# Attention and gated convolution on one core: the convolution's middle tap moved into the sigmoid's scale, the norm's gain into x, first loads on another queue, a new order, and unread products in TensorE's early waits

## The chip, the cores and the metric

The kernel runs on one core of a Trainium2 chip. The metric is device time in microseconds (us), as the median of several runs. The core has a TensorE (matrix products, PE in the profile), a VectorE (DVE), a ScalarE (ACT), a GpSimd (POOL) that here issues most loads, and a SyncE (SP) that here issues transfers only. Each engine takes its instructions strictly in its own order and waits on semaphores for others. Matrix products are written to PSUM, eight banks of 2 KB per partition; everything else lives in SBUF, 128 partitions wide.

## What is computed

Eight batches, 8 heads, 576 positions, 64 numbers per head, so a model width of 512; the gated layer is 1024 wide.

```
kv  = einsum('bhsd,bhse->bhde', k, v)            # no softmax
o   = einsum('bhsd,bhde->bhse', q, kv)
o   = o / sqrt(mean(o*o, -1) + 1e-6) * g_norm    # per head, g_norm has 64 entries
x   = o.transpose(0, 2, 1, 3).reshape(8, 576, 512)
h   = relu(x @ w_in)                             # 512 -> 1024
c   = w0*h[s-1] + w1*h[s] + w2*h[s+1]            # per feature, zero at both ends
out = (h * sigmoid(c)) @ w_out                   # 1024 -> 512
```

All inputs and the output are fp32; inside, operands of products are bf16.

## The kernel before

Everything is kept transposed, features on partitions and positions along the free axis: a batch of x is 4 tiles of 128 x 576, a batch of h is 8 tiles of 128 x 576. The kernel is a set of small steps, each a function with one to a dozen instructions, and a text, ORDER, that lists them one after another by name and numbers (`hm.3.4` is step `hm` for batch 3, feature tile 4). A loop at the end runs through that text, so the order of the instructions on each engine is written out by hand; dependencies between engines are found by the framework, and a buffer pool hands out buffers in turn, waiting until the oldest of its kind is free. Names and lines that matter below:

- `load` (line 148): q, k, v of a batch through GpSimd's queue, which converts fp32 to bf16 on the way. Batch 0 takes q whole and k, v by two heads. `load_w_in` (158): w_in in three parts, kept fp32 in `w_stage`, one of them through SyncE; `ws` (261, VectorE) multiplies by g and converts to `w_in_sb`. `Lw` (256) loads w_out.
- `kv` (272): 64 x 64 products per head pair, 12 per pair and tile; `kvc` (284, 286) copies them into a block-diagonal `kvbd`. `qt` (296) transposes q on TensorE, 24 products per step; `qc` (303, VectorE) copies out. `ot` (308, 309) makes o, 64 and 512 columns.
- Batch 0 has its own norm: `sq` (326), `on` (a product with a matrix of ones), `nl` (348, reciprocal root on ScalarE), `mu0` (357, the product into x, reading in a strided order). The later batches: `sq` (328) and `oc` (334) on ScalarE, `ss` (373), `ln` (383), `sl` (391 to 394, VectorE), `sp` (403, TensorE spreads the factor over 128 partitions), `mu` (409, VectorE: x = o times the factor).
- `hm` (426): eight products of 288 columns into `h_ps`; `re` (432, ScalarE): relu to h.
- The convolution goes by six groups of batches, CONV: 0; 1; 2 and 3; 4 and 5; 6; 7. Batch 0 ('P') runs on TensorE: `di` (480) builds 24 diagonal matrices, `cv` (492) multiplies with them, six products per feature tile, `sv` (500) is the sigmoid, `mv` (506) the gating product. The others ('D') run on VectorE by pairs of feature tiles: `ta` (451) makes three scaled copies of h per tile, `ad` (458, 459) adds them with a shift of one position, `sg` (465, ScalarE) is one sigmoid per pair, `mg` (471) multiplies h in place. Two `tap` buffers take turns.
- `om` (516): eight products of 512 columns per 128 output rows, `ea` (522, ScalarE) copies out, `st` (532) stores through SyncE. Batches go in twos here: 9 row blocks for each.
- PSUM: pool 'a' has three tiles of two banks (for `qt`, `ot`, `hm`, `sp`, `cv`), pool 'b' two of one bank (`kv`, `ss`, `om`).

Of the kernel before, what the change touches and what calls it, by code (L numbers as in the profile page):

```python
# [58 lines left out]
CONV = {0: (0, 1, 'P'), 1: (1, 1, 'D'), 2: (2, 2, 'D'), 3: (4, 2, 'D'), 4: (6, 1, 'D'), 5: (7, 1, 'D')}  # L59
BUFS = {'a': 3, 'b': 2, 'q': 2, 'k': 2, 'v': 2, 'qT': 5, 'sq': 8, 'o32': 8, 'xT': 2, 'h': 2, 'tap': 2, 'row': 8, 'w': 2, 'gate': 3}  # L60

ORDER = """
di.4 di.7 di.6 qt.0.0 qc.0.0 qt.0.1 kv.0.0.1 kvc.0.0.1.0 kvc.0.0.1.1 ot.0.0 di.5 kv.0.1.1 sq.0.0 qc.0.1 on.0
di.2 kvc.0.1.1.0 nl.0 kvc.0.1.1.1 ot.0.1 sq.0.1 kv.0.2.1 on.1 kvc.0.2.1.1 mu0.0 kvc.0.2.1.0 di.1 Lk.1
Lv.1 nl.1 kv.0.3.1 ot.0.2 kvc.0.3.1.1 sq.0.2 on.2 kvc.0.3.1.0 nl.2 mu0.1 ot.0.3 sq.0.3 on.3 ws.1 Lq.1
ws.2 mu0.2 nl.3 ws.0 mu0.3 hm.0.0 hm.0.7 re.0.7 re.0.0 kv.1.0.4 kvc.1.0.4.0 Lw hm.0.5 Lk.2 Lv.2 Lq.2
re.0.5 hm.0.2 re.0.2 qt.1.0 kvc.1.0.4.1 hm.0.4 re.0.4 qc.1.0 ot.1.0 qt.1.1 qc.1.1 ot.1.1 sq.1.0 oc.1.1 sq.1.1
ot.1.2 sq.1.2 di.0 ot.1.3 sq.1.3 oc.1.3 oc.1.2 ss.1 ln.0 hm.0.1 Lk.3 re.0.1 Lv.3 hm.0.6 di.3 Lq.3 oc.1.0
hm.0.3 cv.0.0 re.0.6 sl.0 sp.1.0 mu.1.0 re.0.3 sv.0.0 cv.0.4 sp.1.1 kv.2.0.4 sv.0.4 Lk.4 sp.1.3 mu.1.1
kvc.2.0.4.1 mv.0.0 mu.1.3 sp.1.2 mu.1.2 cv.0.6 cv.0.2 sv.0.6 hm.1.0 mv.0.6 qt.2.1 sv.0.2 mv.0.4 mv.0.2 qc.2.1  # L70
kvc.2.0.4.0 hm.1.1 re.1.0 re.1.1 ot.2.3 ta.1.0 cv.0.7 sq.2.3 sv.0.7 hm.1.4 Lv.4 oc.2.3 cv.0.5 qt.2.0 ta.1.1
ad.1.0 re.1.4 sv.0.5 sg.1.0 hm.1.5 re.1.5 qc.2.0 ot.2.1 mg.1.0 cv.0.1 sq.2.1 sv.0.1 oc.2.1 ot.2.0 sq.2.0
oc.2.0 kv.3.0.4 kvc.3.0.4.0 ta.1.4 Lq.4 qt.3.0 qc.3.0 hm.1.6 hm.1.7 kvc.3.0.4.1 ta.1.5 mv.0.7 re.1.6 re.1.7
ot.3.0 oc.3.0 sq.3.0 mv.0.1 qt.3.1 cv.0.3 qc.3.1 ot.3.3 sv.0.3 oc.3.3 ta.1.6 Lk.5 Lv.5 ta.1.7 ot.3.2 sq.3.3
sq.3.2 ot.3.1 oc.3.2 mv.0.3 ot.2.2 kv.4.0.4 sq.3.1 sq.2.2 oc.3.1 hm.1.2 ss.2 re.1.2 ss.3 ad.1.3 ln.1 
kvc.4.0.4.0 Lq.5 qt.4.1 qt.4.0 ad.1.2 mv.0.5 qc.4.1 hm.1.3 qc.4.0 kvc.4.0.4.1 om.0.2 re.1.3 oc.2.2 sl.1 sp.2.0
mu.2.0 sg.1.3 sp.3.2 mu.3.2 sp.2.2 om.0.0 mu.2.2 mg.1.3 sp.2.3 ot.4.2 Lk.6 Lv.6 mu.2.3 ea.0.2 sp.2.1 om.0.3
mu.2.1 oc.4.2 ot.4.3 sq.4.2 ea.0.0 ta.1.2 sp.3.3 mu.3.3 sq.4.3 oc.4.3 sp.3.0 mu.3.0 ta.1.3 kv.5.0.4 sg.1.2
sp.3.1 kvc.5.0.4.0 hm.2.0 hm.2.5 ea.0.3 mu.3.1 ad.1.1 re.2.0 re.2.5 hm.2.4 qt.5.0 kvc.5.0.4.1 re.2.4 qc.5.0
sg.1.1 qt.5.1 qc.5.1 hm.2.2 re.2.2 ot.4.1 oc.4.1 sq.4.1 st.0.0 mg.1.2 hm.3.4 re.3.4 Lq.6 Lk.7 Lv.7 Lq.7 mg.1.1  # L80
hm.3.5 re.3.5 ot.5.3 oc.5.3 sq.5.3 hm.3.2 hm.3.3 re.3.2 ot.5.0 hm.2.3 ta.2.4 re.3.3 sq.5.0 ta.2.5 re.2.3
ot.5.2 sq.5.2 oc.5.0 oc.5.2 om.0.4 ot.4.0 ta.2.2 ot.5.1 hm.3.6 oc.4.0 ad.2.2 ta.2.3 sq.5.1 ea.0.4 sq.4.0
om.0.5 ss.4 ss.5 oc.5.1 re.3.6 qt.6.0 ea.0.5 ln.2 qt.7.0 qt.6.1 ad.2.1 qc.6.0 om.0.8 ea.0.8 sg.2.1 qc.6.1
om.0.1 sl.2 sp.4.0 ea.0.1 sp.4.2 qc.7.0 sp.5.1 kv.6.0.4 mu.4.0 hm.3.0 mu.5.1 mu.4.2 mg.2.1 sp.5.0 hm.3.1
mu.5.0 re.3.0 re.3.1 sp.4.3 kv.7.0.4 kvc.7.0.4.0 kvc.6.0.4.0 sp.5.3 kvc.7.0.4.1 hm.2.1 re.2.1 mu.4.3 ta.2.0
hm.2.6 sp.4.1 st.0.8 mu.5.3 kvc.6.0.4.1 sg.2.2 sp.5.2 ta.2.1 mu.4.1 om.0.7 hm.3.7 re.2.6 ad.2.0 mg.2.2 re.3.7
sg.2.0 mu.5.2 om.0.6 hm.2.7 re.2.7 hm.4.0 ea.0.6 hm.5.1 ta.2.6 re.5.1 hm.4.3 re.4.3 ta.2.7 ea.0.7 hm.5.0
re.5.0 re.4.0 hm.5.5 re.5.5 hm.5.2 re.5.2 st.0.3 ad.2.3 mg.2.0 st.0.7 qt.7.1 hm.4.1 hm.5.4 sg.2.3 re.4.1
qc.7.1 re.5.4 hm.4.5 re.4.5 hm.4.2 ot.6.1 re.4.2 ta.3.0 oc.6.1 hm.5.3 sq.6.1 mg.2.3 ot.6.3 om.1.5 ot.6.0
re.5.3 ot.7.1 oc.6.3 sq.6.3 ea.1.5 ot.6.2 sq.6.0 oc.7.1 om.1.2 ta.3.1 ta.3.2 oc.6.0 ta.3.3 ad.3.0 ot.7.3  # L90
oc.6.2 sq.6.2 ea.1.2 st.0.6 om.1.6 ot.7.0 sq.7.1 hm.4.4 om.1.8 sg.3.0 re.4.4 ea.1.6 sq.7.0 sq.7.3 ot.7.2
st.1.2 ad.3.1 sq.7.2 ea.1.8 oc.7.3 om.1.3 ea.1.3 ss.6 ss.7 ln.3 hm.5.6 st.0.1 mg.3.0 ta.3.4 re.5.6 ta.3.5
ad.3.2 om.1.4 hm.4.7 st.0.5 om.1.0 oc.7.2 sl.3 oc.7.0 st.1.5 sp.6.0 mu.6.0 sp.6.3 re.4.7 mu.6.3 sg.3.1
ea.1.4 hm.4.6 re.4.6 sp.7.0 mu.7.0 hm.5.7 re.5.7 sp.6.2 om.1.7 st.0.4 ea.1.0 mg.3.1 sp.7.3 ea.1.7 mu.6.2
# [14 lines left out]
def kernel(  # L109
# [11 lines left out]
    nc = tc.nc  # L121
# [8 lines left out]
    NF = D_ff // P  # L130
    eps = 1e-6
# [4 lines left out]
    loads = pool("loads", 2)  # L136
    work = pool("work", 2)
    ps_a = pool("ps_a", BUFS["a"], space=PSUM)
    ps_b = pool("ps_b", BUFS["b"], space=PSUM)


    qkv = {}

    def load(name, b, h0=0, n=H):
        src = {"q": q, "k": k, "v": v}[name]
        if (name, b) not in qkv:
            qkv[name, b] = loads.tile([PS, H, R * D], BF16, name=name + "_sb", bufs=BUFS[name])
# [53 lines left out]
    for t in kvbd:  # L201
        nc.vector.memset(t, 0.0)
# [375 lines left out]
```

## Time and profile before

| | us |
|---|---|
| median of 3 runs | 203.81 (203.37 to 204.84) |
| span of the profiled execution | 201.0 |
| TensorE busy | 175.3 (87%) |
| VectorE busy | 155.3 (77%) |
| ScalarE busy | 145.9 (73%) |
| GpSimd busy | 25.4 (13%) |

The span goes from the first to the last instruction of one profiled execution; all durations come from that one. Busy time alone does not say what sets the end: an engine can be full in one stage and wait in another. So three views are read below: slices of the span (a digit is the busy tenth of a slice), the chain of waits followed back from the last instruction (start, length, what), and the busy time of each engine between two points in time. In lists of instructions, `out<-in` gives tiles by name, then partitions x elements and type, then how many were merged into the line (`x6`); the length of a merged line runs from the first start to the last end. Two instructions in a row on one engine overlap a little at their ends, so the distance from start to start is shorter than a duration.

The largest groups, busy us and mean ns of one:

| line, engine | what | number | us | ns |
|---|---|---|---|---|
| 426 PE | h_ps, 288 columns | 512 | 69.9 | 291 |
| 516 PE | om_ps, 512 columns | 278 | 64.1 | 379 |
| 451 DVE | taps, 576 / 1152 elements | 72 / 48 | 22.2 / 21.6 | 371 / 514 |
| 458 + 459 DVE | adds, 1150 / 2300 elements | 24 / 16 | 18.2 / 21.7 | 757 / 1358 |
| 409 DVE | x = o times factor, 576 | 28 | 20.1 | 749 |
| 432 ACT | relu, 576 | 64 | 41.0 | 656 |
| 465 ACT | sigmoid, 1152 / 2304 | 12 / 8 | 14.0 / 17.1 | 1163 / 2138 |
| 492 PE | products with diagonals | 48 | 10.8 | 286 |

### The profile page before, as it was taken

To read this page: it belongs to the slowest core of one execution; us is meant where nothing else is said; L and a number is where in the kernel's file an instruction comes from. 1 tells how busy PE (TensorE), PEld (TensorE's weight loads), DVE (VectorE), ACT (ScalarE), POOL (GpSimd) and SP (SyncE) were. 2 spreads that over 40 slices of the span, in tenths; PEclk is the share of its full clock that TensorE was granted. 3 is DMA by queue.
4 is the path that set the end of the run, shared out by engine and by line. 5 is a ranking of instruction groups with operands and counts; after the bars stand their busy time and mean duration, and the time that the engine had idled before them with its cause. 6 is when DMAs were issued, how large, how long until landed. Compare 5 with 4: busy or idle time off the path is not lost.

```text
span 201.0 us, 4350 instructions
## 1 busy us (share of the span) xinstructions
PE 175.3 (87%) x1783; PEld 111.8 (56%) x1801; DVE 155.3 (77%) x325; ACT 145.9 (73%) x222; POOL 25.4 (13%) x38
## 2 busy tenths in 40 slices
PE   0057299799998999999999999999999999999792
PEld 0043057477775657766575776445667774444340
DVE  3097921458879799799899999989799999999400
ACT  2006516995999979999678899999978865684532
POOL 7373403103132303100000000000000000000000
PEclk9999999999999999999999999999999999999999
DMA  5999999999999999970200020070005001423654
GB/s 120 146 221 306 198 205 205 204 203 204 204 190 185 201 203 207 202 119 3 104 5 3 0 104 3 7 306 2 3 0 209 3 0 51 159 108 118 247 229 188
DMA packets 26295, 27.03 MB, mean 134 GB/s; under 512 B 1292, under 2 KB 21284, under 8 KB 26276
## 3 DMA queue, kind: packets, MB, share of 16 engines
q0 software_dynamic: 20368, 16.78, 52.4%
q1 hardware_dynamic: 5908, 9.98, 13.1%
q8 instruction: 14, 0.23, 0.4%
q14 instruction: 5, 0.04, 0.1%
HBM read 32.52 MB, written 9.44 MB: 209 GB/s over the span
## 4 chain that ended last, share of the span: by engine, by line
PE 59%; DVE 22%; DMA 10%; ACT 5%; issue 2%; POOL 1%; DVEq 0%; POOLq 0%; ACTq 0%
PE h_ps L426 25%; PE om_ps L516 18%; DVE tap L451 8%; DMA w_stage<-in_moe_w_in_dram 5%; DMA q_sb<-in_q_dram 5%; DVE h L471 4%; PE qt_ps L296 4%; DVE tap L459 3%; PE kv_ps L272 3%; PE sp_ps L403 3%; DVE tap L458 3%; PE cv_ps L492 3%; DVE xT L409 2%; PE o_ps L309 2%; ACT tap L465 2%
## 5 line engine op out<-in xcount | busy, mean ns | idle before, releaser
L426 PE MATMUL h_ps<-xT,w_in_sb 128*128 128x288 bf16 x512 | 69.9, 291 | 3.1 <-DVE w_in_sb L261 2.4
L516 PE MATMUL om_ps<-w_out_sb,h 128*128 128x512 bf16 x278 | 64.1, 379 | 1.5 <-DVE h L471 1.0
L426 PEld LDWEIGHTS <-w_in_sb 128*128 128x128 bf16 x512 | 49.9, 99 | 18.8 <-DVE w_in_sb L261 2.5
L432 ACT ACTIVATE h<-h_ps 128x576 bf16<-128x576 f32 x64 | 41.0, 656 | 14.9 <-PE h_ps L426 14.5
L516 PEld LDWEIGHTS <-h 128*128 128x128 bf16 x288 | 28.0, 98 | 32.2 <-DVE h L471 1.5
L451 DVE TENSOR_SCALAR tap<-h,cw 128x576 bf16<-128x576 bf16 (+1 forms) x120 | 43.8, 428 | 1.8 <-ACT h L432 1.3
L522 ACT ACTIVATE row<-om_ps 128x512 f32<-128x512 f32 x36 | 22.1, 618 | 15.6 <-PE om_ps L516 13.1
L465 ACT ACTIVATE tap<-tap 128x1152 bf16<-128x1152 bf16 (+1 forms) x20 | 31.1, 1553 | 1.6 <-DVE tap L459 1.5
L409 DVE TENSOR_TENSOR xT<-o,sp_ps 128x576 bf16<-128x576 f32 x28 | 20.1, 749 | 5.0 <-PE sp_ps L403 4.8
L471 DVE TENSOR_TENSOR h<-h,tap 128x1152 bf16<-128x1152 bf16 (+1 forms) x20 | 19.8, 992 | 1.8 <-ACT tap L465 1.8
L459 DVE TENSOR_TENSOR tap<-tap 128x1150 bf16<-128x1150 bf16 (+1 forms) x20 | 20.1, 1004 | 0.7
L303 DVE COPY qT<-qt_ps 128x1152 bf16<-128x1152 bf16 x16 | 11.8, 754 | 11.1 <-PE qt_ps L296 10.9
L458 DVE TENSOR_TENSOR tap<-tap 128x1150 bf16<-128x1150 bf16 (+1 forms) x20 | 19.8, 991 | 0.0
L328 ACT ACTIVATE sq<-o_ps 128x576 bf16<-128x576 f32 x28 | 18.2, 689 | 0.5 <-PE o_ps L309 0.5
L334 ACT ACTIVATE o<-o_ps 128x576 f32<-128x576 f32 x28 | 18.1, 677 | 0.5 <-ACT row L522 0.5
L286 ACT ACTIVATE kvbd<-kv_ps 64x256 bf16<-64x256 f32 (+1 forms) x18 | 6.0, 339 | 12.2 <-PE kv_ps L272 11.8
L148 POOL DMA_DIRECT2D k_sb<-in_k_dram x11 | 8.0, 723 | 35.9 <-PE kv_ps L272 35.9
L296 PE MATMUL qt_ps<-ident,q_sb 96*64 96x96 bf16 x384 | 11.2, 217 | 1.4 <-DMA q_sb<-in_q_dram 1.1
L296 PEld LDWEIGHTS <-q_sb 96*64 96x64 bf16 x384 | 9.6, 117 | 3.3 <-issue 2.1
L403 PE MATMUL sp_ps<-wparts,spread 128*128 128x288 bf16 x56 | 9.8, 286 | 0.2 <-DVE xT L409 0.2
L272 PEld LDWEIGHTS <-k_sb 96*64 96x64 bf16 x384 | 8.0, 123 | 3.3 <-issue 3.3
L309 PE MATMUL o_ps<-qT,kvbd 128*128 128x512 bf16 x25 | 9.6, 407 | 0.0
(55 smaller groups left out, 114.9 us busy)
## 6 DMA issues: line engine op xcount, KB each, us to landing
out_dram<-row SPq DMA_DIRECT2D x36, 256.0 KB, 2.3
q_sb<-in_q_dram POOLq DMA_DIRECT2D x8, 576.0 KB, 12.6
k_sb<-in_k_dram POOLq DMA_DIRECT2D x7, 576.0 KB, 11.3
v_sb<-in_v_dram POOLq DMA_DIRECT2D x7, 576.0 KB, 13.6
w_stage<-in_moe_w_in_dram POOLq DMA_DIRECT2D x1, 1024.0 KB, 9.9
w_out_sb<-in_moe_w_out_dram POOLq DMA_DIRECT2D x1, 1024.0 KB, 19.9
k_sb<-in_k_dram POOLq DMA_DIRECT2D x4, 144.0 KB, 9.4
v_sb<-in_v_dram POOLq DMA_DIRECT2D x4, 144.0 KB, 9.2
```

Source lines behind the costliest of these rows:

```text
L296: nc.tensor.transpose(ps[i * D:(i + 1) * D, tt, r * PS:(r + 1) * PS], q_sb[:, 2 * (2 * u + tt) + i, r * D:(r + 1) * D], ident[:PS, :PS])
L328: nc.scalar.activation(s.rearrange("p (n r) -> p n r", r=R), natural(src), AX.Square)
L409: nc.vector.tensor_mul(x_tile(b)[:, t, :].rearrange("p (e n) -> p e n", e=2), T["o32", b, t].rearrange("p (e n) -> p e n", e=2), T["sp", b ...
L426: nc.tensor.matmul(ps[:, e, :HS], w_in_sb[:, t, f * P:(f + 1) * P], x[:, t, e * HS:(e + 1) * HS], start=(t == 0), stop=(t == NT - 1))
L432: nc.scalar.activation(h_tile(b // 2)[:, f, b % 2, :].rearrange("p (e n) -> p e n", e=2), T["hm", b, f][:, :, :HS], AX.Relu)
L451: nc.vector.tensor_scalar_mul(tap[:, m, f % 2, :, :].rearrange("p b s -> p (b s)"), h_tile(p)[:, f, bs, :].rearrange("p b s -> p (b s)"), ...
L458: nc.vector.tensor_add(tap[:, 1, :, 1:], tap[:, 1, :, 1:], tap[:, 0, :, :S - 1])
L459: nc.vector.tensor_add(tap[:, 1, :, :S - 1], tap[:, 1, :, :S - 1], tap[:, 2, :, 1:])
L465: nc.scalar.activation(tap, tap, AX.Sigmoid)
L471: nc.vector.tensor_mul(h, h, T["tap", c, j][:, 1])
L516: nc.tensor.matmul(ps, h[:, f, m * P:(m + 1) * P], w_out_sb[:, f, :], start=(f == 0), stop=(f == NF - 1))
L522: nc.scalar.activation(T["os", p, m], T["om", p, m], AX.Copy)
```

## The change

**The convolution.** Batch 0 no longer runs on TensorE; its 48 products, the 24 diagonal matrices and their steps are gone, and all six groups run on VectorE. The middle tap w1 is taken out of the sum: a preparation step `pc` divides w0 and w2 by w1 (w1 held away from zero), `ta` makes two scaled copies instead of three, `aa` adds these two with their shifts, `ab` adds h itself, and the sigmoid multiplies by w1 through its per-partition scale operand. Since that operand belongs to one feature tile, there is now one sigmoid per feature tile instead of one per pair. The two tap buffers are fixed tiles with rows of 584 and a zeroed column on either side of what is written.

**g.** The factor g leaves w_in and goes into x: `mu` and `mu0` become three-operand instructions (o times g times factor). So w_in is loaded as bf16 by GpSimd's queue in two halves, without a staging tile or rescale. `mu0` reads in plain order, because the copy of batch 0's transposed q (`qc0`, now on ScalarE) puts the positions in order.

**First loads.** Heads 0 to 3 of q, k and v of batch 0 come as fp32 through SyncE's queue, six transfers of 295 KB, and are converted by `ca` (k, v on VectorE, q on ScalarE). Heads 4 to 7 come through GpSimd's queue by two heads, batch 1 in halves, then w_in. The small transfers of the convolution's weights and g are issued by ScalarE. w_out comes in two halves, after batches 2 and 3.

**Order and buffers.** ORDER is new throughout. Each buffer is now named in it: `hm.0.0@0` takes slot 0 of its kind, so the pool no longer chooses. The numbers of slots are as before. `om` of the first and the last pair of batches is split into two steps of four products. Batch 5 is taken before batch 4.

**Unread products.** `fi` multiplies a tile of zeros by itself, 128 x 512, into a PSUM tile that nobody reads: 20 of them, six at the very start and the rest between the steps of batch 0's attention and up to the first `hm`.

The diff's core (the order, the pools' plumbing and unchanged arithmetic left out):

```diff
-CONV = {0: (0, 1, 'P'), 1: (1, 1, 'D'), 2: (2, 2, 'D'), 3: (4, 2, 'D'), 4: (6, 1, 'D'), 5: (7, 1, 'D')}
+CONV = {0: (0, 1), 1: (1, 1), 2: (2, 2), 3: (4, 2), 4: (6, 1), 5: (7, 1)}
...
+        T["stg"] = ring("h", [PS, 3, 2, 2, R * D], FP32, name="stg")
+        for t in range(2):
+            for x in "kvq":
+                nc.sync.dma_start(out=T["stg"][:, "kvq".index(x), t], in_=heads(x, 0, 2 * t, 2))
...
+        for t in range(2, NT):
+            for x in "kvq":
+                nc.gpsimd.dma_start(out=qkv[x, 0][:, 2 * t:2 * t + 2, :], in_=heads(x, 0, 2 * t, 2))
...
+    def fi(n, r):
+        ps = ring(r, [P, 512], FP32, name="fi_ps", padded_shape=[P, {"a": 1024, "b": 512}[r]])
+        for _ in range(n):
+            nc.tensor.matmul(ps, zero[:, :P], zero, start=True, stop=True)
...
+    def pc():
+        c1 = slice(NF, 2 * NF)
+        tmp = consts.tile([P, 3, NF], FP32, name="ctmp")
+        nc.vector.tensor_copy(cw, T["cw"])
...
+        nc.vector.reciprocal(tmp[:, 2], cw[:, c1])
+        nc.vector.tensor_mul(cw[:, 0:NF], cw[:, 0:NF], tmp[:, 2])
+        nc.vector.tensor_mul(cw[:, 2 * NF:], cw[:, 2 * NF:], tmp[:, 2])
...
-    def ws(i):
-        lo, hi = W_COLS[i]
-        nc.vector.tensor_scalar_mul(w_in_sb[:, :, lo:hi], w_stage[:, :, lo:hi], g_sb[:, 0:1])
...
+    def ca(x, t):
+        to, fr = qkv[x, 0][:, 2 * t:2 * t + 2, :], T["stg"][:, "kvq".index(x), t]
+        if x == "q":
+            nc.scalar.activation(to, fr, AX.Copy)
+        else:
+            nc.vector.tensor_copy(to, fr)
...
     def mu(b, t):
-        nc.vector.tensor_mul(
+        nc.vector.scalar_tensor_tensor(
             x_tile(b)[:, t, :].rearrange("p (e n) -> p e n", e=2),
-            T["o32", b, t].rearrange("p (e n) -> p e n", e=2), T["sp", b, t][:, :, :HS])
+            T["o32", b, t].rearrange("p (e n) -> p e n", e=2), g_sb[:, 0:1], T["sp", b, t][:, :, :HS],
+            op0=AL.mult, op1=AL.mult)
...
     def ta(c, f):
...
-        for m in range(3):
-            col = m * NF + f
-            nc.vector.tensor_scalar_mul(
-                tap[:, m, f % 2, :, :].rearrange("p b s -> p (b s)"),
-                h_tile(p)[:, f, bs, :].rearrange("p b s -> p (b s)"), cw[:, col:col + 1])
+        nc.vector.tensor_scalar_mul(tap[:, 0, f % 2, :n, 8:8 + S], h[:, f], cw[:, f:f + 1])
+        nc.vector.tensor_scalar_mul(tap[:, 1, f % 2, :n, :S], h[:, f], cw[:, 2 * NF + f:2 * NF + f + 1])
...
-        nc.vector.tensor_add(tap[:, 1, :, 1:], tap[:, 1, :, 1:], tap[:, 0, :, :S - 1])
-        nc.vector.tensor_add(tap[:, 1, :, :S - 1], tap[:, 1, :, :S - 1], tap[:, 2, :, 1:])
+        nc.vector.tensor_add(tap[:, 1, :, :n, :S], tap[:, 0, :, :n, 7:7 + S], tap[:, 1, :, :n, 1:1 + S])
...
+        nc.vector.tensor_add(y, y, h[:, 2 * j:2 * j + 2])
...
-    def sg(c, j):
+    def sg(c, f):
         act_table("sig")
-        tap = T["tap", c, j].rearrange("p m f b s -> p m (f b s)")[:, 1, :]
-        nc.scalar.activation(tap, tap, AX.Sigmoid)
+        y = T["tap", c, f // 2][:, 1, f % 2, :CONV[c][1], :S]
+        nc.scalar.activation(y, y, AX.Sigmoid, scale=cw[:, NF + f:NF + f + 1])
```

## The prediction

> **What bounds it now.** I read the page's slices first, then the chain of waits at both ends, then the stages by engine.
>
> The slices (40 of 5.03 us, busy tenths):
>
> ```profile
> PE   0057299799998999999999999999999999999792
> DVE  3097921458879799799899999989799999999400
> ACT  2006516995999979999678899999978865684532
> DMA  5999999999999999970200020070005001423654
> ```
>
> TensorE (PE) is full from slice 6 on, VectorE (DVE) from slice 18, ScalarE (ACT) in slices 11 to 15, and the DMA engines from slice 1 to 16. The chain of waits (start, us, what) says what the ends hang on:
>
> ```profile
> 1.29 9.51 DMA q_sb<-in_q_dram
> ...
> 12.59 9.87 DMA w_stage<-in_moe_w_in_dram
> 22.48 1.29 DVE w_in_sb L261
> ...
> 25.53 4.02 PE h_ps L426 x16
> 29.55 1.33 PE kv_ps L272 x25
> 30.89 2.07 PE h_ps L426 x16
> ...
> 188.69 8.82 PE om_ps L516 x40
> 197.54 0.60 ACT row L522
> ```
>
> So 25.5 us pass until the first h_ps product: two loads and a rescale. The first 16 take 4.02 us, the next 16 take 2.07. At the end the last product stops at 197.5 and 3.5 us of copy and store follow. Busy time by stage (start:end, length, then PE, PEld, DVE, ACT, POOL, each with its instructions; clock; DMA share; GB/s):
>
> ```profile
> 8.00:14.00 6.00, 2.72 (x61) 2.49 (x61) 4.06 (x19) 0.22 (x1) 2.81 (x4) 1.00 1.31 200
> 25.50:50.00 24.50, 22.81 (x296) 16.12 (x299) 10.79 (x24) 15.72 (x28) 3.83 (x5) 1.00 1.30 204
> 50.00:70.00 20.00, 18.54 (x325) 13.38 (x328) 16.91 (x37) 19.80 (x35) 5.50 (x7) 1.00 1.29 195
> 143.00:189.00 46.00, 44.66 (x268) 26.29 (x271) 44.24 (x90) 33.88 (x46) 0.00 (x0) 1.00 0.23 86
> ```
>
> PE carries the middle, DVE (44.2 of 46.0) the stage before the tail, ACT (19.8 of 20.0) the stage from 50 to 70. Costs are taken as start-to-start pitches, since durations overlap:
>
> ```profile
> 159.73 1.76 DVE L451 TENSOR_SCALAR tap<-h,cw 128x576 bf16<-128x576 bf16 x6
> 161.41 0.75 DVE L471 TENSOR_TENSOR h<-h,tap 128x1152 bf16<-128x1152 bf16 x1
> 162.08 0.75 DVE L458 TENSOR_TENSOR tap<-tap 128x1150 bf16<-128x1150 bf16 x1
> 162.86 0.76 DVE L459 TENSOR_TENSOR tap<-tap 128x1150 bf16<-128x1150 bf16 x1
> 163.53 1.76 DVE L451 TENSOR_SCALAR tap<-h,cw 128x576 bf16<-128x576 bf16 x6
> ```
>
> A tap of 576 is 0.28 (1.68/6); an add is 0.78 when the next one reads it, else 0.67. Likewise from the chain: h_ps 0.98 per eight, om_ps 1.73 per eight, sp_ps 0.25 a pair, 24 transposes 0.63, 48 kv products 0.88; relu, square and copy 0.545 each, row 0.49, sigmoid of 1152 1.06 and of 2304 2.02, x product 0.66, tap of 1152 0.43, adds of 2304 1.38 and 1.27.
>
> **A check of the method.** From the first h_ps product the old order holds 162.7 us of PE work at these pitches; the trace took 172.0 (25.5 to 197.5). The 9.3 lost lie 5.6 before 50 us (cold products, loads), 2.1 from there to 143, 1.5 after. From 50 to 70 ACT, 99% busy, got through 18.1 us of pitch-work in 20.0: pressed, it delivers 0.905.
>
> **The change, part by part.**
>
> PE. The 48 conv products of batch 0 go: 8 x 0.74 = 5.9 us. The halved om_ps groups hold the same 288 products. From the first h_ps product on, 155.8 us remain; all fills lie before it.
>
> DVE. Each pair of features loses two scalings and keeps two adds and a product. For 12 one-batch pairs that is 2 x 0.28 = 0.56 each, for 8 two-batch pairs 2 x 0.43 = 0.86: 13.6 less. Batch 0 now runs here: 4 x (4 x 0.28 + 0.78 + 0.67 + 0.67) = 13.0 more, against 8 gate products of 0.39 and two late diagonal groups, 4.2 less. Setup of 2.3 (spread matrix, group sums) moves behind the start. The x product becomes a three-operand one: the trace has it only at 288 elements, 0.518 us (line 394). By its fixed part (0.518 less 288 elements at the x product's pace, about 0.22) 576 take 0.82 and pitch 0.74; by doubling, 1.04. No gain is possible, as it does the old product and one more. I take 0.74, because casts and products of other sizes here also split into a fixed part and a slope: 28 x 0.08 = 2.2 more (10.6 at the other end). The first add now reads both inputs at odd offsets; lines 458 and 459 each have an odd one and stay at 0.67, so I take 0.78 in sum; the bound is the x product's unpacked pace, 1.26 and 2.46: 18 us more over 24 pairs; the lower end is none, the sizes being equal. Strided rows of 584 I cost at nothing by the same adds. DVE from the first h_ps product: 136.3, as before (136.5), but it can now begin where it idled (10.8 of 24.5).
>
> ACT. A sigmoid per feature instead of per pair: slope (2.02 - 1.06)/1152 gives 0.48 for 576, plus 0.10 fixed, plus 0.09 for a per-partition operand (line 348 with a bias 0.740, line 326 without 0.648): 0.67, bounds 0.58 and 0.77. Two-batch: 1.15. Per pair that is 0.28 more in either size, 20 x 0.28 = 5.6, and batch 0 pays 8 x (0.67 - 0.545) = 1.0; a halved kv copy adds 0.3. ACT from the first h_ps product: 130.9 becomes 137.8; table loads stay at eight. Four of ACT's early kv copies go to DVE (4 x 0.16), which has 8 us of work in the opening and is idle for the rest.
>
> Start. SyncE loads 6 x 0.295 MB fp32; at the 323 GB/s of 2 to 3 us, when SyncE's first load ran, 5.5 us, so all in by 7.5. GpSimd's queue then carries, up to the first half of w_in: 0.88 (heads 4 to 7) + 0.88 (half of batch 1) + 0.52 = 2.29 MB at the 200 GB/s of 8 to 14 us, 11.5 us: 19.0. The rescale of w_in (about 2.8 of DVE) is gone, so the first h_ps product starts at 19.5 instead of 25.5. Bounds: 17.5 if a megabyte slips in early, 23.5 if PE is cold (rival 2). Batch 0's attention hides under it: per tile ACT needs 0.6 + 0.65 + 0.74, four tiles 8 us plus two casts from about 6, so 16. ACT issues three small DMAs (0.5 to 0.6 each, lines 176 and 178) before its table load: done by 3.7, before q. The select ahead of GpSimd's loads costs 0.3, under SyncE's transfers. Six fills run in PE's idle first 4 us, fourteen (3.0 us warm) in waits.
>
> Here a rule speaks against the SyncE loads. The Trainium skill, "DMA: Bandwidth & Descriptors", section "Anatomy of one DMA — SWDGE (gpsimd) path", fits 2.0 us + bytes/436 GB/s, an estimate of 3.4 us for the 0.59 MB q load, so the early gain would be near nothing; the trace shows 9.51, and the measurement decides.
>
> What is late next: after w_in's first half the queue brings 0.88 + 0.52 + 1.77 + 1.77 + 1.05 = 6.0 MB at 200 GB/s up to the second half of w_out: 49.0. The om_ps product that needs it has 25.1 us of PE in front: 44.6. So 4.4 of the 6.0 won come back as a wait for loads. In the new order, work in front of a step, from the first h_ps product:
>
> | step | PE | ACT | DVE |
> |---|---|---|---|
> | second half of the first om_ps | 25.1 | 27.6 | 25.1 |
> | sp_ps of batch 7, tile 3 | 107.9 | 107.9 | 104.7 |
> | last five om_ps groups | 147.1 | 135.3 | 136.3 |
>
> The three engines run level for 100 us. With ACT never a hold: 49.0 + (107.9 - 25.1) = 131.8. With ACT at 0.905 from 20.5 on: 20.5 + 107.9/0.905 = 139.7. Behind it come 47.9 of PE, 1.5 lost as before, 3.5 of tail: 184.7 or 192.6. I go two thirds of the way, as the stage at 0.905 is the only one with ACT that full: span 190.0. The profiled span of 201.0 stands 2.8 under the median 203.81, and I carry that over: 193.0, rounded up.
>
> The named buffers keep the old numbers of PSUM (three pairs and two banks), so by themselves they cost nothing here; what the new order may cost is rival 3. SyncE's stores stand behind six loads that end 50 us before the first store. GpSimd's w_out stands behind batches 2 and 3 now, and its price is the 4.4 above.
>
> **Rivals.**
>
> 1. Forecast, 187 to 197: chance 0.58.
>
> 2. The fills do not warm PE. For: transposes before 13 us ran at 44 ns (48 in 2.13), later 26; granted clock reads 1.00 throughout, so it does not show this. Cold, PE's opening is 18.8 us instead of 9.9, the fills alone 20 x 0.43 = 8.6, on the path from about 6: start 23.5, first products cold, 2 more. Loads have arrived by then, so om_ps gets its half at 50.6 to 52, not 49: some 3.5 over the forecast, 196.5, and up to 201. Chance 0.13. The Trainium skill, "TensorE: Matmul & The Clock Gate", Part 1, says half rate until about 3.4 us of sustained work; by it six fills (2.6 us) and a gap would leave PE cold, an estimate that favours this rival.
>
> 3. Slower: DVE waits at its gate product. Per pair it finishes the sum, ACT does two sigmoids (1.33 or 2.28) behind whatever is queued, and with two tap buffers DVE has one other pair (2.6 to 4.4 us) to fill the time. In 24 pairs a wait w each makes DVE the bound: 19.5 + 2 + 5 (loads) + 136.3 + 12.3 (five om_ps groups, tail) + 24w = 175.1 + 24w. It overtakes the forecast at w = 0.6 and the old time at 1.1; at 1.4 it gives 208.7 span, 211.5. Against: 20 pairs now lose 1.8 us in all. For: ACT was never this level with PE. Chance 0.17; stopping near 1.0, so 201.8 to 205.8: 0.08.
>
> 4. Better than the forecast, under 187: ACT holds nothing, loads come 2 us early. Chance 0.04.
>
> **The numbers.** About 1% is what a measurement here can tell: 201.8 to 205.8 counts as no change. Faster 0.58 + 0.13 + 0.04 = 0.75, same 0.08, slower 0.17. The dear bounds on DVE alone (odd offsets 18, three operands 8.4) give spans of 193.1 and 183.5, both together 201.5, so 204.3 in time, within the range. Range 185 to 205: some 0.02 below, 0.18 above.
>
> **What would show it.** First h_ps product near 19.5 with 16 in about 2.1; three-operand x products at 0.82; sigmoids of 576 at 0.76 each; the middle at 90% or more on all three engines; PE waiting for w_out or kv loads before 50; five om_ps groups and 3.5 us at the end. The forecast fails if DVE's wait for sigmoids totals over 10 us, if the first h_ps product comes after 24, or if adds of 1152 take 1.3.

## The result, and the profile after

| | before | after |
|---|---|---|
| median, us | 204.06 (203.37 to 204.84, 4 runs) | 193.8 (192.08 to 194.33, 4 runs) |
| ratio to before | | 0.9498 (0.9444 to 0.9553) |
| span of the profiled execution | 201.0 | 189.9 |
| first h_ps product | 25.5 | 24.3 |
| TensorE work from there on, lost in it | 162.7, 9.3 | 155.8, 6.0 |
| tail behind the last product | 3.5 | 3.8 |

The 11.1 us of span are 1.2 of start, 6.9 of TensorE work and 3.3 of lost time, less 0.3 of tail. The profiled execution of the changed kernel is the fastest of its four (192.08; the spans of the other three are 191.4 to 192.3), and further down the profiles of the run with the middle tap back in the sum (206.16) and of the run with more copies on ScalarE (207.07) are of executions 2.0 and 3.1 us slower than the medians of these runs. The slices of the changed kernel (4.75 us each):

```profile
PE   5078898899899999999999999999999999999992
DVE  4134679997988999999899999999989895887100
ACT  2047669999998999999998999999995779478431
DMA  5999999999999995989910000441040010170974
```

From the seventh slice on three engines are nearly full, not one: before, VectorE stood at 1 to 5 in slices 6 to 9. The two ends of the chain of waits:

```profile
3.44 10.77 DMA stg<-in_q_dram
14.23 0.85 ACT q_sb L314
...
24.46 0.99 PE h_ps L480 x8
...
170.59 15.55 PE om_ps L537 x72
186.14 0.02 issue
186.16 0.60 ACT row L543
```

The start hangs on the second q load through SyncE, which lands at 14.2, and on ten us of attention behind it. At the end 72 products of the last layer run without a gap. Busy time by stage, columns as in the prediction:

```profile
24.30:49.30 25.00, 23.22 (x337) 15.99 (x335) 22.67 (x48) 22.99 (x42) 6.11 (x8) 1.00 1.30 205
49.30:138.40 89.10, 87.92 (x979) 56.56 (x979) 84.39 (x126) 86.54 (x136) 6.99 (x9) 1.00 0.66 119
112.00:138.40 26.40, 26.27 (x230) 14.51 (x225) 25.16 (x34) 25.97 (x40) 0.00 (x0) 1.00 0.19 71
138.40:186.20 47.80, 47.73 (x280) 27.15 (x278) 32.27 (x62) 32.33 (x54) 0.00 (x0) 1.00 0.33 123
```

In the first 25 us behind the first h_ps product VectorE now does 22.7 where it did 10.8 in 24.5, and from 49.3 to 138.4 PE, DVE and ACT stand at 99, 95 and 97%. The groups of the changed convolution and x product (line, engine, what; busy, mean ns; idle time before, and for what):

```profile
L521 ACT ACTIVATE taps<-taps,cw 128x576 bf16<-128x576 bf16 x32 | 23.5, 775 | 1.0 <-DVE taps L515 0.9
L469 DVE SCALAR_TENSOR_TENSOR xT<-o,g_sb,sp_ps 128x576 bf16<-128x576 f32 x28 | 21.3, 810 | 1.8 <-PE sp_ps L463 1.8
L521 ACT ACTIVATE taps<-taps,cw 128x1152 bf16<-128x1152 bf16 x16 | 19.4, 1250 | 0.0
L509 DVE TENSOR_TENSOR taps<-taps 128x1152 bf16<-128x1152 bf16 x16 | 12.1, 757 | 0.3
L515 DVE TENSOR_TENSOR taps<-taps,h 128x1152 bf16<-128x1152 bf16 x16 | 12.0, 756 | 0.3
L527 DVE TENSOR_TENSOR h<-h,taps 128x1152 bf16<-128x1152 bf16 x16 | 12.0, 754 | 5.5 <-ACT taps L521 5.5
```

The three-operand product takes 0.810, the adds at odd offsets 0.757, the sigmoid 0.775, and the gate products of one-batch pairs (L527) wait 5.5 us for sigmoids in all. The opening, by its timeline (start, length, engine, line):

```profile
9.50 0.84 ACT L314 ACTIVATE q_sb<-stg 96x768 bf16<-96x768 f32 x1 [5.56 <-DMA stg<-in_q_dram]
12.52 1.06 PE L236 MATMUL fi_ps<-zero 128*128 128x512 bf16 x2
14.23 0.84 ACT L314 ACTIVATE q_sb<-stg 96x768 bf16<-96x768 f32 x1 [0.82 <-DMA stg<-in_q_dram]
24.30 2.12 PE L480 MATMUL h_ps<-xT,w_in_sb 128*128 128x288 bf16 x16
```

ScalarE waits 5.56 us for the first q through SyncE and has the second only at 14.2. TensorE still runs at half pace at 12.5 (two unread products in 1.06; later 0.61) and at full pace by the first h_ps (16 in 2.12).

### The profile page after: what moved, and what is told of

It reads as the page before. It is cut to its first block, busy times and chain, and to the rows that moved or that the text cites. A ratio compares the mean times of both kernels' runs of the same rounds, so it can differ in the third digit from the quotient of the medians.

```text
span 189.9 us, 4293 instructions
## 1 busy us (share of the span) xinstructions
PE 173.9 (92%) x1773; PEld 106.6 (56%) x1773; DVE 149.0 (78%) x280; ACT 153.2 (81%) x246; POOL 25.9 (14%) x39
## 4 chain that ended last, share of the span: by engine, by line
PE 64%; DMA 11%; DVE 11%; ACT 9%; issue 2%; SPq 1%; POOL 0%; ACTq 0%
PE om_ps L537 28%; PE h_ps L480 23%; DMA stg<-in_q_dram 6%; DMA v_sb<-in_v_dram 5%; PE qt_ps L352 4%; PE sp_ps L463 3%; ACT sq L397 3%; PE kv_ps L328 2%; ACT h L488 2%; DVE taps L502 2%; DVE taps L509 2%; DVE taps L515 2%; PE o_ps L383 2%; DVE taps L503 2%; ACT o L402 1%
## 5 line engine op out<-in xcount | busy, mean ns | idle before, releaser
L537 PE MATMUL om_ps<-w_out_sb,h 128*128 128x512 bf16 x288 | 66.7, 379 | 0.1
L521 ACT ACTIVATE taps<-taps,cw 128x576 bf16<-128x576 bf16 (+1 forms) x48 | 42.9, 933 | 1.0 <-DVE taps L515 0.9
L543 ACT ACTIVATE row<-om_ps 128x512 f32<-128x512 f32 x36 | 21.8, 605 | 10.7 <-PE om_ps L537 10.4
L527 DVE TENSOR_TENSOR h<-h,taps 128x1152 bf16<-128x1152 bf16 (+1 forms) x24 | 22.7, 953 | 5.7 <-ACT taps L521 5.7
L509 DVE TENSOR_TENSOR taps<-taps 128x1152 bf16<-128x1152 bf16 (+1 forms) x24 | 23.0, 958 | 0.5
L515 DVE TENSOR_TENSOR taps<-taps,h 128x1152 bf16<-128x1152 bf16 (+1 forms) x24 | 22.9, 956 | 0.5
L469 DVE SCALAR_TENSOR_TENSOR xT<-o,g_sb,sp_ps 128x576 bf16<-128x576 f32 x28 | 21.3, 810 | 1.8 <-PE sp_ps L463 1.8
L502 DVE TENSOR_SCALAR taps<-h,cw 128x576 bf16<-128x576 bf16 (+1 forms) x48 | 20.6, 428 | 1.5 <-ACT h L488 1.4
L503 DVE TENSOR_SCALAR taps<-h,cw 128x576 bf16<-128x576 bf16 (+1 forms) x48 | 20.9, 436 | 0.0
L352 PE MATMUL qt_ps<-ident,q_sb 96*64 96x96 bf16 x384 | 11.5, 210 | 7.1 <-ACT q_sb L314 7.0
L383 PE MATMUL o_ps<-qT,kvbd 128*128 128x512 bf16 x32 | 12.0, 387 | 0.0
L377 DVE COPY qT<-qt_ps 128x1152 bf16<-128x1152 bf16 x14 | 10.4, 754 | 1.8 <-PE qt_ps L352 1.6
L285 POOL DMA_DIRECT2D q_sb<-in_q_dram x8 | 6.0, 748 | 33.5 <-PE qt_ps L352 29.2
## 6 DMA issues: line engine op xcount, KB each, us to landing
v_sb<-in_v_dram POOLq DMA_DIRECT2D x6, 576.0 KB, 12.6
q_sb<-in_q_dram POOLq DMA_DIRECT2D x6, 576.0 KB, 12.3
w_in_sb<-in_moe_w_in_dram POOLq DMA_DIRECT2D x2, 512.0 KB, 12.5
```

Of the source, the lines that this page charges most:

```text
L352: nc.tensor.transpose(ps[i * D:(i + 1) * D, r * PS:(r + 1) * PS], qkv["q", b][:, 2 * t + i, r * D:(r + 1) * D], ident[:PS, :PS])
L502: nc.vector.tensor_scalar_mul(tap[:, 0, f % 2, :n, 8:8 + S], h[:, f], cw[:, f:f + 1])
L503: nc.vector.tensor_scalar_mul(tap[:, 1, f % 2, :n, :S], h[:, f], cw[:, 2 * NF + f:2 * NF + f + 1])
L509: nc.vector.tensor_add(tap[:, 1, :, :n, :S], tap[:, 0, :, :n, 7:7 + S], tap[:, 1, :, :n, 1:1 + S])
L515: nc.vector.tensor_add(y, y, h[:, 2 * j:2 * j + 2])
L521: nc.scalar.activation(y, y, AX.Sigmoid, scale=cw[:, NF + f:NF + f + 1])
```

## The experiments

The account that the runs test: three engines run level, the convolution's products taken from TensorE pay because VectorE has room for them, the early loads buy nothing, and the unread products do warm TensorE. A, B and C in an expectation are named anew for each run. Medians taken at different times are compared through their ratios to the kernel before; 0.01 is 2.04 us.

**The unread products left out.**

```diff
     def fi(n, r):
-        for _ in range(n):
+        for _ in range(0):
```

> The changed kernel without the 20 unread products. Theory A (they warm TensorE): the granted clock, 0.50 from 8 to 14 us in the changed kernel and 1.00 from 15, stays at half into the first h_ps products; these start about 1 us earlier than 24.3 (less work in front) but the first 16 take 4.0 us instead of 2.1, and later steps of the opening run cold: time 1 to 3 us longer, 194.8 to 196.8. Rival B (they only take room): 1.4 us of them lie on the chain of waits before the first h_ps product, so 1 to 1.5 us shorter, 192.3 to 192.8.

Measured 194.88, ratio 0.9589 (0.9541 to 0.9636): 1.9 us more than with them, with intervals that overlap a little (1.4 more against the changed kernel's second measurement, 0.9521). The timeline:

```profile
25.15 1.17 PE L352 MATMUL qt_ps<-ident,q_sb 96*64 96x96 bf16 x24
26.26 3.78 PE L480 MATMUL h_ps<-xT,w_in_sb 128*128 128x288 bf16 x16
```

Without them 24 transposes take 1.17 (0.70 in the runs that are warm by then) and the first 16 h_ps products 3.78 instead of 2.12, which alone is 1.66. So the unread products do warm TensorE in time for the first layer, and the time is A's. The first h_ps product came no earlier than with them, as A had it, but at 26.26; the last section shows how far it scatters.

**GpSimd held back until SyncE's third load has landed.**

```diff
+        gate = consts.tile([PS, 1], FP32, name="gate")
+        nc.gpsimd.tensor_copy(gate, T["stg"][:, 2, 0, 0, 0:1])
         for t in range(2, NT):
```

> The changed kernel, but GpSimd first reads one element of the third SyncE load (q, heads 0 and 1), so that its own loads start only when that has landed. Theory A (the SyncE loads are late because GpSimd's converting loads share the DMA engines): the third lands near 5.5 instead of 9.5 us and the sixth near 8 instead of 14.2, the first h_ps product comes at 20 to 21 instead of 24.3, and 2 to 4 us of the total go. Rival B (SyncE's queue has its own slow pace at the start): the third still lands near 9, GpSimd's loads start there, the first h_ps product comes at 26 to 28 and the time is 2 to 5 us longer.

Measured 194.43, ratio 0.9581 (0.952 to 0.9641). The third load landed at 8.45 instead of 9.50, the sixth by 12.3 instead of 14.2. Windows of this run, in which GpSimd has no loads under way, only SyncE, and ScalarE its three small ones:

```profile
2.00:4.00 2.00, 2.00 (x5) 0.45 (x3) 0.41 (x7) 1.28 (x1) 0.00 (x0) 1.00 0.94 272
4.00:6.00 2.00, 0.01 (x1) 0.00 (x0) 1.11 (x2) 0.00 (x0) 0.00 (x0) 1.00 0.58 145
6.00:8.00 2.00, 0.00 (x0) 0.00 (x0) 0.00 (x0) 0.00 (x0) 0.00 (x0) 1.00 0.94 274
```

Without GpSimd's loads the queue moves 272, 145 and 274 GB/s in these stretches, 230 on the mean, where the prediction counted on 323. The third load comes one us earlier than in the first profile of the changed kernel; the rest of its lateness is not GpSimd's doing. So B's reading is the nearer one, though the time is 1.7 us longer (0.9581 less 0.9498) and not 2 to 5. The first h_ps came at 25.73, since w_in now starts later.

**No loads through SyncE: batch 0 whole through GpSimd, by two heads, and no conversions.**

```diff
-        T["stg"] = ring("h", [PS, 3, 2, 2, R * D], FP32, name="stg")
-        for t in range(2):
-            for x in "kvq":
-                nc.sync.dma_start(out=T["stg"][:, "kvq".index(x), t], in_=heads(x, 0, 2 * t, 2))
...
-        for t in range(2, NT):
+        for t in range(NT):
```

> The changed kernel with all of batch 0 through GpSimd's queue, by two heads, and no fp32 staging or conversion; this undoes the first loads alone. Theory A (SyncE's first loads win 4 us or more): first h_ps product at 28 or later, time 3 to 5 us longer. Rival B (what they win at their landing is lost to sharing the DMA engines, 13 to 14 us for the sixth): first h_ps product within 1.5 us of 24.3 and the time within 1.5 us of the changed kernel's.

Measured 190.57 (190.34 to 190.79), ratio 0.9374 (0.9343 to 0.9406): the fastest version here, 2.5 us under the changed kernel (0.9498 less 0.9374; 3.0 against its second measurement). Both A and B missed this: A expected a loss, B no difference beyond 1.5 us. Its timeline:

```profile
7.60 0.69 PE L345 MATMUL qt_ps<-ident,q_sb 96*64 96x96 bf16 x12 [3.58 <-DMA q_sb<-in_q_dram]
...
22.16 2.13 PE L473 MATMUL h_ps<-xT,w_in_sb 128*128 128x288 bf16 x16 [0.87 <-DMA w_in_sb<-in_moe_w_in_dram]
```

The first transposes start at 7.6, not 10.4, and h_ps waits for w_in, the limit that the prediction had in mind, at 22.2. So the change's early loads, with the conversions that they need, cost 2.5 to 3 us.

**Half of SyncE's loads: heads 0 and 1 only.**

```diff
-        for t in range(2):
+        for t in range(1):
             for x in "kvq":
                 nc.sync.dma_start(out=T["stg"][:, "kvq".index(x), t], in_=heads(x, 0, 2 * t, 2))
...
-        for t in range(2, NT):
+        for t in range(1, NT):
```

> Only heads 0 and 1 of q, k and v come through SyncE (three transfers instead of six), heads 2 to 7 through GpSimd. Theory A (SyncE's transfers land late because GpSimd's share the DMA engines with them, and fp32 brings more bytes by that queue; half of them cost half): third transfer lands at 7 to 9, first h_ps product at 22.5 to 24, time 191 to 192.5, between the kernel without SyncE loads (190.6) and the changed one (193.8). Theory B (the early start is a gain if it is kept short): third transfer lands by 6, first h_ps product by 22, time 189.5 to 190.6.

Measured 191.79, ratio 0.9429 (0.9384 to 0.9474), between the two, as A has it; but the third load landed at 9.6 and not at 7 to 9, no earlier than with six, so three loads less behind it on SyncE (and three more on GpSimd) do not help it. The first h_ps came at 24.07.

**Without SyncE's loads, and without the unread products.**

```diff
-        for _ in range(n):
+        for _ in range(0):
```

> The kernel that loads batch 0 through GpSimd alone, now also without the unread products. The output is not changed by it. Theory A (the unread products warm TensorE, and batch 0's attention waits on cold products otherwise): first sixteen h_ps products in over 3 us instead of about 2.1, first h_ps product up to 2 later than 22.2, time 191.5 to 193.5 against 190.6. Theory B (with q there early, TensorE's own work warms it, and the unread products only stand in its way): first h_ps product no later than 22.2, time 189.5 to 190.6.

Measured 191.91, ratio 0.9428 (0.939 to 0.9466). The timeline:

```profile
22.00 3.71 PE L473 MATMUL h_ps<-xT,w_in_sb 128*128 128x288 bf16 x16
...
25.89 0.70 PE L345 MATMUL qt_ps<-ident,q_sb 96*64 96x96 bf16 x24
```

The start comes no later (22.00; B had that right), since it waits for w_in, but the 16 products are cold again, and 1.1 us are lost, as A has it (the intervals overlap a little). So the unread products delay nothing, and save the cold first products.

**The pool choosing buffers in turn again,** same numbers of buffers, without SyncE's loads.

```diff
-        return p.tile(shape, dtype, name=name, tag=f"{r}{s}", bufs=1, **kw)
+        return p.tile(shape, dtype, name=name, tag=r, bufs=N[r], **kw)
```

> The kernel that loads batch 0 through GpSimd alone, with the pool choosing among the same numbers of buffers in turn instead of the names in the order. Theory A (named buffers are worth nothing by themselves, as the prediction took them): within 1 us of 190.6. Theory B (in the new order the buffers' turns come at the wrong time, and some steps wait for a buffer that is still read): 192.5 to 197, with new waits of h_ps, tap or x tiles on their last readers.

Measured 191.41, ratio 0.94 (0.9373 to 0.9428), 0.5 us over the run with names, with intervals that overlap, as A has it. Named buffers by themselves are worth nothing that these runs can tell.

**The changed kernel with the middle tap back in the sum** (three scalings, one sigmoid for a pair, the weights not divided), all else as changed.

```diff
+        nc.vector.tensor_scalar_mul(tap[:, 2, f % 2, :n, :S], h[:, f], cw[:, NF + f:NF + f + 1])
...
-        nc.vector.tensor_add(y, y, h[:, 2 * j:2 * j + 2])
+        nc.vector.tensor_add(y, y, T["tap", c, j][:, 2, :, :n, :S])
```

> The changed kernel with the middle tap back in the sum: three scaled copies per feature tile, the second add reads the third copy, one sigmoid per pair without a scale. VectorE 32 x 0.28 + 16 x 0.43 = 15.8 us more, ScalarE about 6.6 less. Theory A (the freed VectorE time is needed, as in the old kernel's stage from 143 to 189): VectorE had 13 us of idle time between 24.3 and 176.9 and half a microsecond of slack at the end, so 6 to 12 us longer, 200 to 206. Rival B (TensorE alone sets the end, or ScalarE does): within 2 us of 193.8.

Measured 204.16, ratio 1.0022 (0.9989 to 1.0056): the whole gain is gone, within A's range. One window of it:

```profile
50.00:143.00 93.00, 87.59 (x1011) 55.83 (x1010) 88.61 (x149) 82.01 (x124) 8.24 (x11) 0.98 0.63 113
```

VectorE is now the fullest (88.6 of 93), and TensorE waits for its small products (5.3 us at sp_ps). The added work is 24 pairs with two more scalings: 16 x 0.56 + 8 x 0.86 = 15.8 us; 10.7 of it shows in the time, though ScalarE was relieved.

**The old kernel with the middle tap in the sigmoid's scale** and the preparation of the weights for it. The first tap's shift is left out, so that the old buffers serve.

```diff
-        for m in range(3):
+        for m in (0, 2):
...
+        for f in (2 * j, 2 * j + 1):
+            tap = T["tap", c, j][:, 1, f % 2].rearrange("p b s -> p (b s)")
+            nc.scalar.activation(tap, tap, AX.Sigmoid, scale=cw[:, NF + f:NF + f + 1])
```

> The old kernel with the middle tap taken out of the sum for the batches on VectorE: two scaled copies, two adds, a sigmoid per feature tile with the weight as its scale. The shift of the first tap is left out, so the output differs; numbers and sizes of the instructions are as they would be. VectorE 13.6 us less, ScalarE 5.6 more. Theory A (the old kernel is bound by TensorE up to 143 us and loses only 1.5 us to VectorE after): 0 to 2.5 us shorter, 201.5 to 204. Rival B (VectorE was the old kernel's bound): 6 or more shorter, under 198. Rival C (ScalarE, 99% busy from 50 to 70, cannot take more): 1 to 4 longer.

Measured 204.44, ratio 1.0064 (1.0035 to 1.0094). The stage from 70 to 143 us, first of the kernel before, then of this run:

```profile
70.00:143.00 73.00, 72.41 (x749) 47.29 (x755) 67.81 (x104) 66.11 (x98) 2.30 (x3) 1.00 0.42 89
```

```profile
70.00:143.00 73.00, 72.70 (x752) 46.93 (x751) 61.24 (x88) 67.80 (x107) 2.30 (x3) 1.00 0.43 90
```

and of the same run the timeline of TensorE behind VectorE's last gate product:

```profile
189.88 7.30 PE L530 MATMUL om_ps<-w_out_sb,h 128*128 128x512 bf16 x33 [0.69 <-DVE h L485]
```

VectorE loses 6.6 us of work there and TensorE, full before and after, goes no faster. In the stage behind it, where VectorE was the second fullest engine before (44.24 of 46.0, TensorE 44.66), the relief buys nothing either:

```profile
143.00:190.00 47.00, 45.85 (x278) 26.88 (x276) 40.53 (x73) 37.16 (x57) 0.00 (x0) 1.00 0.23 84
```

VectorE has dropped to 40.53 of 47.0 and TensorE stays full; the last five groups start at 189.9 instead of 188.7, behind a gate product and its sigmoids. The time is 1.3 us longer, which is C's size, but not C's place: the first h_ps product is 0.4 late already (25.93 for 25.53), ReLUs at 68.93 and 88.36 are 0.56 and 0.54 late, so the stage from 50 to 70, where ScalarE was fullest, loses almost nothing, and the rest comes later. Relief for an engine that does not hold the pace buys nothing.

**The old kernel with less TensorE work:** batch 0's convolution on TensorE cut to its middle tap (16 of 48 products stay; the side taps of batch 0 are left out).

```diff
-        for m in (1, 0, 2):
+        for m in (1,):
...
-                                 start=(m == 1), stop=(m == 2))
+                                 start=True, stop=True)
```

> The old kernel with batch 0's convolution on TensorE cut to its middle tap: 16 of 48 products stay, 3.9 us of TensorE work go, and ScalarE and VectorE keep theirs; the side taps of batch 0 are left out of the output. Theory A (TensorE sets the pace): 3 to 3.9 us shorter, about 200. Rival B (ScalarE, full in that stage, sets it): within 1.5 us of 204.

Measured 201.81, ratio 0.9967 (0.9908 to 1.0026), although 3.9 us of products are gone. The window in which they were:

```profile
50.00:70.00 20.00, 17.57 (x316) 12.21 (x315) 16.94 (x38) 19.88 (x35) 5.50 (x7) 1.00 1.30 198
```

TensorE falls from 18.54 to 17.57, ScalarE stays full (19.88 of 20). The first h_ps product comes at 25.99 (before 25.53), the last five groups at 188.31 (before 188.69), so 0.8 of the 3.9 us come through in this execution. In the old order ScalarE held this stage, as the prediction read it and B has it; by the interval of the ratio up to 1.9 us of gain are not excluded. That an order which spreads ScalarE's work would let the 3.9 through is argued; no run shows it by itself.

**The changed kernel with 27 more unread products,** three ahead of each of nine steps of the last layer for batches 2 and 3.

```diff
-... qc.7.1@3 om.1.1.0@0 ...
+... qc.7.1@3 fi.3.b@0 om.1.1.0@0 ...
```

> The changed kernel with 27 more unread products of 512 columns, three in front of each om_ps group of the second pair of batches, about 110 to 134 us: 27 x 0.216 = 5.8 us of TensorE work and nothing else. Theory A (TensorE sets the pace of the middle): the whole 5.8 us come on top, 199.6. Rival B (ScalarE and VectorE, level with TensorE in the prediction's sums, hold it there): 0 to 3 us.

Measured 201.85, ratio 0.9878 (0.9789 to 0.9967). One group by the timeline:

```profile
118.08 0.81 PE L236 MATMUL fi_ps<-zero 128*128 128x512 bf16 x3
118.94 1.89 PE L537 MATMUL om_ps<-w_out_sb,h 128*128 128x512 bf16 x8
```

and the stretch that holds most of them:

```profile
114.00:140.00 26.00, 25.53 (x241) 13.68 (x234) 20.94 (x29) 21.52 (x35) 0.00 (x0) 1.00 0.19 72
```

A group takes 0.86 from start to start, nine 7.7; the time grew by 7.8 (0.9878 less 0.9498; the two intervals leave it open by some 2 either way). The stretch from the first h_ps product (26.68) to the end of the last product took 169.4, against 161.8 and 162.3 in the two profiles of the changed kernel: 7.2 to 7.6 more. All of it came on top, as A has it; A's 5.8 had counted 0.216 for a product, and a group of three took 0.86.

**The changed kernel with 18 more copies on ScalarE,** two at each of the same nine places.

```diff
+    def fa(n):
+        for _ in range(n):
+            nc.scalar.activation(junk, zero, AX.Copy)
...
-... qc.7.1@3 om.1.1.0@0 ...
+... qc.7.1@3 fa.2 om.1.1.0@0 ...
```

> The changed kernel with 18 more copies on ScalarE (128 x 512 bf16, about 0.45 to 0.5 from start to start, 8 to 9 in sum), two at each of the nine places where the run with more unread products had its three. The output is not changed by them. Theory A (ScalarE runs level with TensorE in that stretch and is pressed, as the prediction's table has it: 107.9 of work in front of the same step for both): most of it comes on top, +5 to +9, time 199 to 203. Theory B (only TensorE sets the pace there, and ScalarE's idle time between its instructions can take the copies): under +2, time 193 to 196. The stretch from the first h_ps product to the last om_ps product is compared with 161.8 and 162.2, so that the opening's scatter does not count.

Measured 204.01, ratio 1.0031 (0.9994 to 1.0068). One pair by the timeline:

```profile
119.91 1.28 ACT L247 ACTIVATE junk<-zero 128x512 bf16<-128x512 bf16 x2
121.10 0.58 ACT L549 ACTIVATE row<-om_ps 128x512 f32<-128x512 f32 x1
```

and the stretch:

```profile
115.00:140.00 25.00, 20.17 (x186) 11.01 (x188) 19.30 (x26) 24.77 (x41) 0.00 (x0) 1.00 0.20 74
```

Two copies take 1.19, so 18 are 10.7 (the expectation had counted 8 to 9), and the ratios differ by 10.9 us (1.4 either way by the intervals): again all of it, beyond the top of A's range by the mis-sized copy. The stretch from the first h_ps product to the end of the last one took 174.5 in the profiled execution (207.07), 12.2 to 12.6 more. Read the last windows together: as changed, PE, DVE and ACT stand at 26.3, 25.2 and 26.0 of 26.4; with more products, at 25.5, 20.9 and 21.5 of 26; with more copies, at 20.2, 19.3 and 24.8 of 25. Whichever of TensorE and ScalarE gets more work stays full, and the others drop back.

**The changed kernel once more.**

> The changed kernel once more, unaltered, beside the three variants, for a second look at its opening. Theory A (the start varies from run to run by where SyncE's and GpSimd's first loads meet; the rest is fixed): time 193 to 195, first h_ps product somewhere between 24 and 27, and from it to the last om_ps product 161 to 163 us as in the first profile. Theory B (the first profile was typical in its opening too): first h_ps product within 0.5 of 24.3. If the stretch after the first h_ps product differs by more than 2 us, neither holds.

Measured 194.03 (193.01 to 194.24), ratio 0.9521 (0.9484 to 0.9558). First h_ps at 25.88, and 162.3 us from it to the end of the last product (161.8 in the first profile), as A has it: the opening varies, what follows does not.

## Why the prediction came out right

The time was right (193.0 for 193.8, span 190.0 for 189.9), but not all of its steps. A late start and two stretches that were shorter than forecast cancelled, and that they did so to a tenth of a us of span is luck.

- **Right: TensorE's work sets the scale.** 162.7 to 155.8 was the largest single term, and the last stage kept to it: 47.7 busy of 47.8.
- **Right: the unit costs.** Three-operand product 0.810 for a forecast of 0.82, sigmoids 0.775 for 0.76, adds at odd offsets with the duration of the old ones. The dear ends (1.04, 1.26) did not come.
- **Right: three engines level.** The table with 107.9, 107.9 and 104.7 us of work in front of the same step is what the two load experiments show: more work on TensorE or on ScalarE came on top in full. VectorE, 3.2 lower in the table, had 15.8 added by the third tap, and 10.7 of it showed.
- **Wrong: the start.** "The first h_ps product starts at 19.5"; it came at 24.3 and 25.9, past the 24 that the prediction named as its failure. Its first term, SyncE's six loads "all in by 7.5" at 323 GB/s, was the mis-sized one: the third landed at 9.5, the sixth at 14.2. The rate was read from a moment in which the queue had just begun; without GpSimd's loads it moved 230 GB/s from 2 to 8 us, and 145 in the middle of it. The second term failed too: GpSimd issued w_in's first half at 11.0, after waits, and it took 11.5 to land, so 22.5 instead of 19.0. By the first term the attention, which was to hide under w_in's load, became the path. Without SyncE's loads the start was 22.2, right behind w_in. In the executions that started at 25.9 and later a second cause came on top, TensorE at half pace in that attention (see rival 2).
- **Wrong: the wait for w_out.** "4.4 of the 6.0 won come back as a wait for loads": TensorE waited 0.2 us for loads behind the first h_ps. The second half of w_out landed at 52.9, later still than the 49.0 of the forecast, but the first product that needs it ran at 53.67, 29.4 behind the first h_ps for 25.1 of work: with little won at the start there was nothing to give back.
- **Mis-sized: ScalarE as the hold.** The forecast went two thirds of the way to ScalarE at 0.905: 137.1 - 19.5 = 117.6 from the first h_ps to sp_ps of batch 7, tile 3. The trace has 138.39 - 24.30 = 114.1 for 107.9 of work on each of two engines, so 0.946 with the loads' 0.2 of waits in it. Which of the level engines causes the 6.2 us lost there stays open.

In sum, measured less predicted: start +4.8; from there to sp_ps of batch 7, tile 3, -3.5; from there to the last product 47.7 for 47.9 + 1.5, -1.7; tail +0.3; span -0.1. In the later profile of the same kernel (span 191.9, time 194.02) the start is 6.4 late, the rest up to the last product 162.3 for 167.0, so 4.7 short, and the tail 0.3 long: the span is 1.9 over, and the time 1.0, since the prediction put 3.0 between span and time, with its rounding, and 2.1 lie between them there.

**The rivals.** Rival 2 (cold TensorE) came half true. In the first profile TensorE was cold at 12.5 us and at full pace from 15 on, so its late start had another cause. In the later one it fell back to half pace: the two unread products at 17.81 took 1.03, those at 17.05 in the first profile 0.61.

```profile
17.05 0.61 PE L236 MATMUL fi_ps<-zero 128*128 128x512 bf16 x2
```

```profile
17.81 1.03 PE L236 MATMUL fi_ps<-zero 128*128 128x512 bf16 x2
```

From the sixth load to the first h_ps product it took 10.1 us in the first profile and 11.3 in the later one, and 11.7, 12.5 and 12.5 in the runs with more unread products, with more copies and with three taps, which ran these products in 1.03 too. So the unread products do not keep TensorE warm through batch 0's attention. By the first h_ps it was warm in all five, and the runs without unread products show what cold costs, 1.1 to 1.9. The Trainium skill, "TensorE: Matmul & The Clock Gate", Part 1, gives about 3.4 us of sustained work until full rate; without SyncE's loads the work began at 7.6 and the transposes at 11.79 were still slow (0.61 for twelve; warm 0.45), so here it was somewhat more than four, with gaps between the products. Rival 3 had its mechanism and not its price: 5.7 us of waits for sigmoids over 24 pairs (5.5 of them in the one-batch groups), w = 0.24, where 1.1 would have cost the gain. The rule that spoke against the SyncE loads came out on the right side, but not by its own numbers: the fit of the Trainium skill, "DMA: Bandwidth & Descriptors", section "Anatomy of one DMA — SWDGE (gpsimd) path", left the early gain near nothing, and the runs make it a loss of 2.5 to 3. The same fit gives 2.7 us, an estimate, for the 295 KB of fp32 in a load of two heads through GpSimd (2.3 for the bf16 bytes that land, the count that the prediction used), and in the run without SyncE, where several were under way together, these took 5.1 to 5.4 (the medians for k, v and q).

**Where the gain comes from.** No part has it alone: the middle tap's move in the old kernel 1.0064, fewer products in the old kernel 0.9967, the new order with three taps 1.0022, all together 0.9498. What fits all of these: moving the middle tap makes the room on VectorE for batch 0's convolution, whose products leave TensorE, and the new order starts VectorE and spreads ScalarE early enough that all three stay full. The first half is shown by the run with three taps; the part of the order is argued from the stages, since no run has the middle tap and the fewer products in the old order, or the new order with batch 0's convolution on TensorE. Nor is the move of g, which takes w_in's rescale out of the start, tried by itself. The unread products are worth 1 to 2 us, the SyncE loads take 2.5 to 3 away.

## What to carry to other kernels

When several engines have the same work in front of the same step, load on one of them can cost all of it, as it did here on TensorE and on ScalarE; and where another engine holds the pace, relief buys nothing, as in the old kernel. So a change has to be priced as a whole, by the sum in front of a step on each engine. Size a transfer by a stretch as long and as early as its own, not by the best rate that the profile shows, and ask what else the same DMA engines carry then. A forecast that hits the total can still have wrong terms: check the terms against their own lines, in more than one execution.

## What the hardware showed that was not expected

- **The clock row does not show the first warm-up.** Windows of two executions of the changed kernel, the first line of the first profile and the second of the later one:

```profile
11.50:14.60 3.10, 2.88 (x8) 0.64 (x7) 1.54 (x4) 1.29 (x3) 1.61 (x3) 0.50 1.28 222
```

```profile
8.00:14.60 6.60, 3.64 (x32) 1.61 (x32) 1.60 (x4) 2.14 (x3) 2.31 (x4) 1.00 1.23 247
```

The granted clock reads 0.50 in one and 1.00 in the other, and in both two unread products took 1.06 us there. The clock records of the traces begin with the first change, at 4.6 us in the first profile, 13.3 in the later one and 30.6 in the kernel before, and ahead of it the row reads 1.00 whatever the pace. A fall to half pace behind that is shown; in the later profile:

```profile
16.80:19.80 3.00, 2.94 (x32) 1.32 (x31) 1.48 (x5) 1.24 (x2) 0.07 (x1) 0.50 1.28 205
```

- **SyncE's first two loads land by 4.4 and 5.3, the third at 8.5 to 9.8,** whether six or three are issued and whether GpSimd loads at the same time or not. Why is open.
- **The opening scatters, with TensorE's pace.** With SyncE's six loads and the unread products the first h_ps product came at 24.3, 25.9, 26.7, 26.8 and 27.1 in five profiles (the last three with edits elsewhere). The sixth load landed between 14.2 and 15.0 in all of them, and TensorE was at half pace for the longer behind it the later the product came. What sends TensorE back to half pace, or keeps it there, is not shown. Without SyncE's loads the product came at 22.2, 22.0 and 21.9. The times of these three kernels lay within 0.45, 1.29 and 0.31 us, those of the changed kernel within 2.3 and 1.2, so the early loads are not the only source of scatter.
